# Attention and MoE on one core: squares stored in longer runs, the tile table worked out in place, the last chunk's closing dealt out, the last puts behind the branch

## Chip, core and metric

One core of a Trainium2 chip. The metric is the device time in microseconds of one execution. The engines are TensorE (PE; PEld are its weight loads), VectorE (DVE), ScalarE (ACT), GpSimd (POOL) and SyncE (SP, which here issues nearly all DMAs except the indirect ones, which are POOL's).

## The reference

```python
# attention: u, v (8, 2496, 256), z (8, 2496, 64)
scores = (1.0 / S) * np.matmul(z, z.transpose(0, 2, 1))
x = (u * np.matmul(np.maximum(scores, 0.0) ** 2, v)).reshape(B * S, D)
# MoE: N = 19968 rows, D = 256, E = 8 experts, F = 1024
logits = x @ w_gate + modality_bias[modality_id]
e_idx = np.argmax(logits, axis=1)
probs = np.exp(logits - logits.max(-1, keepdims=True))
probs /= probs.sum(-1, keepdims=True) + 1e-09
gate_w = probs[np.arange(N), e_idx]
for e in range(E):
    mask = e_idx == e
    h = np.maximum(x[mask] @ w1[e], 0.0)
    out[mask] = gate_w[mask, None] * (h @ w2[e])
```

## The kernel before

Every fp32 number of a product is split into a high and a low part in the fp32r type, and three matmuls (high x high, low x high, high x low) are summed.

**Phase 1, attention** (to 1275 us). For each of 8 batches the 2496 queries are taken in 5 chunks of 512 (the last has 448), and for each chunk the keys in 10 steps, 400 steps in all. A step makes scores s (L312), takes relu on ACT (r, L320), squares it (L366), splits the square into ah (`high`, L390, on DVE or ACT) and al (`low`, L399, DVE), and multiplies both with v into acc (L423). The square of the scores is symmetric, so 158 of the steps have their counterpart elsewhere: DVE transposes them in 32 x 32 blocks (`turn_squares`, L337, tile turn), SP stores them to DRAM (`store_squares`, L349, and L353 for a chunk's last step, i = 9), and the counterpart loads them (`load_turned`, L329) instead of computing scores. A planner with a cost for each piece ("piece" on an engine, "transfer" on SP with its number of issues) writes the order of each engine's queue.

When a chunk is done, its closing follows: the sum leaves PSUM, `weigh_u` (L490) multiplies by u, `rows_part` (L502 on ACT, L504 on DVE) and `rows_rest` (L508) make three bf16 parts, `make_rows` (L519) multiplies them by a constant matrix on PE (rows of x and gate logits), `take_rows` (L529, L530) copies those out and `take_gates` (L537) sums the logits. Routing of a batch follows: `route_logits` (L553 to L563), `route_exp` (L569), `route_places` (L577 to L598, which ends in cnt, the counts of each expert), `route_count` (L607, two small matmuls on cnt into pc), `route_gates`, `route_slots`, and `scatter` (L643, POOL) puts rows of x in DRAM by expert (xs).

**Phase 2, MoE.** Tiles of 512 rows of one expert, t = -4 to 34; the first four are tiles that are full for certain before the last batch is routed. For a tile SP fetches rows (xg, `fetch`) and a new expert's weights (wr, `fetch_weights`, split on ACT, L842, and DVE, L847); DVE transposes the rows (`turn_blocks`, L867), ACT and DVE split them (xh L874, xl L879). Eight slots f = 0 to 7 follow: `up` makes ph with six matmuls (L1246), ACT hh (L1250), DVE hl (L1251). Behind f = 3 stands the closing of the tile before (`close`: down matmuls L1264 and L1270, y on DVE L1317, `put_rows` on POOL, L1284), behind f = 7 the first half of the down matmuls. Four PSUM buffers (ps_h) serve ph, make_rows and pc in turn.

Work of the last chunk and the last batch, and the plan of the tiles (`plan`, which expert and which row each tile has), is put between the slots of tiles -4 to -1 by `put(slot, ...)`: slot n is tile -4 + n // 8, f = n % 8, and the pieces come behind that slot's matmuls. Every engine works its queue in this written order.

**The end.** The last tile's closing and a quarter tile are followed by a nest of branches (L1498, L1499) on the number of tiles left over (nq, none here). POOL issues its puts, goes over the branch, and then come the instructions that end the program (L1552).

## Time and profile before

| | |
|---|---|
| runs of the kernel | 2170.31, 2171.5, 2174.4 us; median 2171.5 |
| profiled execution | 2172.29 us, its span 2170.5 us |
| granted clock of PE, mean of the span | 0.994 |
| busy: PE / DVE / ACT / POOL | 2138.6 / 1644.4 / 1436.3 / 359.4 us |
| DMA | 356.84 MB in 563537 packets, 488818 of them under 512 bytes |

The span runs from the first to the last instruction; the execution's time has 1.8 us around it. PE is busy for 99% of it, so what is of interest is where the remaining time stands, and which engines have room at that place.

### The profile page before, as it was taken

Reading aid. Unit: us, or ns where it says so; the run is one execution under the profiler, and the core shown is the slowest. Engines: PE = TensorE matmul, PEld = TensorE weight load, DVE = VectorE, ACT = ScalarE, POOL = GpSimd, SP = SyncE. Lnnn points to the kernel's source line nnn. Section 1 sums busy time; section 2 is a strip of 40 time slices with the busy share of each in tenths; the row PEclk is TensorE's granted clock in tenths of the full one; section 3 lists DMA queues with packets and bytes.
Section 4 is the critical chain, followed back from the end, with each engine's and each line's share of the span. In section 5 each row is a group of like instructions: output and inputs, shape, how many; then the busy total and the mean of one; then the engine's idle time right before and its main releaser. Section 6 shows DMA issues by size and latency. Waiting matters only on the chain. (4 is left out here: it accounts for less than half of the span.)

```text
span 2170.5 us, 44782 instructions
## 1 busy us (share of the span) xinstructions
PE 2138.6 (99%) x17190; PEld 1858.0 (86%) x17190; DVE 1644.4 (76%) x2309; ACT 1436.3 (66%) x2021; POOL 359.4 (17%) x342
## 2 busy tenths in 40 slices
PE   9999999999999999999999989999999999999996
PEld 7888898888888998899998878888888888888885
DVE  8888889888888888788888865666666666666663
ACT  8779779779678779778688753545454545455452
POOL 0000400300300401301302303211111121212121
PEclk9999999999999999999999999999999999999998
DMA  8975965957957957947957822654545454545440
GB/s 179 260 207 115 238 188 121 260 160 141 271 141 151 287 120 155 280 116 166 264 133 166 248 54 78 200 149 136 156 130 162 124 162 121 161 131 156 137 129 24
DMA packets 563537, 356.84 MB, mean 164 GB/s; under 512 B 488818, under 2 KB 505714, under 8 KB 563314
## 3 DMA queue, kind: packets, MB, share of 16 engines
q1 hardware_dynamic: 548226, 312.82, 56.7%
q0 software_dynamic: 15088, 41.08, 5.4%
q8 instruction: 136, 2.23, 0.4%
q14 instruction: 87, 0.71, 0.1%
HBM read 229.73 MB, written 124.19 MB: 163 GB/s over the span
## 5 line engine op out<-in xcount | busy, mean ns | idle before, releaser
L423 PE MATMUL acc<-ah,vh 64*128 64x512 f32 (+1 forms) x3120 | 459.8, 385 | 2.7 <-ACT x L479 2.0
L423 PE MATMUL acc<-al,vh 64*128 64x512 f32 (+1 forms) x3120 | 448.6, 382 | 0.0
L423 PE MATMUL acc<-ah,vl 64*128 64x512 f32 (+1 forms) x3120 | 447.7, 382 | 0.0
L399 DVE TENSOR_TENSOR al<-r,ah 128x1024 fp32r<-128x1024 f32 (+1 forms) x359 | 421.9, 1186 | 32.5 <-ACT ah L390 24.0
L1251 DVE SCALAR_TENSOR_TENSOR hl<-ph,hh 128x512 fp32r<-128x512 f32 x312 | 210.1, 690 | 277.7 <-ACT hh L1250 232.7
L1246 PE MATMUL ph<-xh,w 128*128 128x512 f32 x1248 | 401.0, 392 | 0.6 <-ACT rb L530 0.6
L643 POOL DMA_INDIRECT xs<-x,sloti x160 | 201.3, 1258 | 1125.4 <-issue 582.1
L423 PEld LDWEIGHTS acc<-ah,vh 64*128 64x128 f32 x3120 | 328.5, 184 | 44.6 <-ACT x L479 4.6
L423 PEld LDWEIGHTS acc<-al,vh 64*128 64x128 f32 x3120 | 331.5, 184 | 36.4
L1250 ACT ACTIVATE hh<-ph 128x512 fp32r<-128x512 f32 x312 | 181.2, 596 | 266.8 <-PE ph L1246 213.0
L423 PEld LDWEIGHTS acc<-ah,vl 64*128 64x128 f32 x3120 | 325.7, 184 | 37.3
L390 ACT CAST ah<-r 128x1024 fp32r<-128x1024 f32 (+1 forms) x271 | 276.6, 1034 | 38.1 <-DMA r<-squares 14.2
L320 ACT ACTIVATE r<-s 128x1024 f32<-128x1024 f32 (+2 forms) x244 | 249.1, 1022 | 79.0 <-PE s L312 71.7
L1264 PE MATMUL po<-w,hh 128*128 128x512 f32 x1248 | 296.2, 389 | 0.0
L1246 PEld LDWEIGHTS ph<-xh,w 128*128 128x128 f32 x1248 | 235.7, 189 | 48.9 <-ACT rb L530 0.8
L1264 PEld LDWEIGHTS po<-w,hh 128*128 128x128 f32 x1248 | 234.0, 188 | 48.3
L1284 POOL DMA_INDIRECT out_dram<-y,ids x157 | 153.0, 975 | 668.8 <-DVE y L1317 633.0
L366 ACT ACTIVATE r<-r 128x1024 f32<-128x1024 f32 (+2 forms) x243 | 255.8, 1053 | 5.6
L1246 PE MATMUL ph<-xl,w 128*128 128x512 f32 x624 | 244.9, 392 | 3.9 <-DVE xl L879 3.9
L337 DVE STREAM_TRANSPOSE turn<-r 128x1024 f32<-128x1024 f32 x158 | 195.8, 1240 | 60.2 <-DMA squares<-turn 32.8
L312 PE MATMUL s<-zm 64*128 64x512 f32 (+1 forms) x1452 | 221.5, 397 | 1.6 <-ACT r L320 1.5
L847 DVE TENSOR_TENSOR w<-wr,w 128x1024 fp32r<-128x1024 f32 x148 | 174.7, 1220 | 17.9 <-ACT w L842 10.0
(162 smaller groups left out, 2021.8 us busy)
## 6 DMA issues: line engine op xcount, KB each, us to landing
wr<-in_moe_w_dram SPq DMA_DIRECT2D x148, 512.0 KB
squares<-turn SPq DMA_DIRECT2D x508, 128.0 KB
r<-squares SPq DMA_DIRECT2D x96, 512.0 KB
r<-squares SPq DMA_DIRECT2D x62, 448.0 KB
ut<-in_ut_dram SPq DMA_DIRECT2D x40, 512.0 KB
xg<-xs SPq DMA_DIRECT2D x156, 128.0 KB
vr<-in_v_dram SPq DMA_DIRECT2D x32, 512.0 KB
squares<-turn SPq DMA_DIRECT2D x186, 64.0 KB
```

The costliest lines, as they stand in the source:

```text
L312: nc.tensor.matmul(out=s[t][:, :w], lhsT=lhs, rhs=mv[halves[t], ql, :w], start=n == 0, stop=n == 2)
L320: nc.scalar.activation(out=r[:, t, :w], in_=s[t][:, :w] if g < 2 else s[:, :, :w], func=AF.Relu, scale=INV)
L337: nc.vector.transpose(out=y.rearrange(order, n=2), in_=st_a[g].rearrange("p n (t i) -> p n t i", i=BLK))
L366: nc.scalar.square(out=a[:, t, :w], in_=r[:, t, :w])
L390: copy(out=ah[:, :, :w], in_=st_a[g][:, :, :w])
L399: nc.vector.tensor_tensor(out=al[:, :, :w], in0=a[:, :, :w], in1=ah[:, :, :w].bitcast(F32), op=ALU.subtract)
L423: nc.tensor.matmul(out=acc[b, c][r][dh][:, :w], lhsT=V[b, k // J][y][halves[r], k % J, dh * P:(dh + 1) * P], rhs=x[halves[r], k % 2, :w], ...
L643: nc.gpsimd.indirect_dma_start(out=xs, out_offset=bass.IndirectOffsetOnAxis(ap=RT[b]["sloti"][:n, k:k + 1], axis=0), in_=x[:n, j, :], in_o ...
L1246: nc.tensor.matmul(out=ph, lhsT=lhs, rhs=rhs[:, k, :], start=n == 0, stop=n == 3 * KD - 1)
L1250: nc.scalar.activation(out=hh, in_=ph, func=AF.Relu)
L1251: nc.vector.scalar_tensor_tensor(out=hl, in0=ph, scalar=0.0, in1=hh.bitcast(F32), op0=ALU.max, op1=ALU.subtract)
L1264: nc.tensor.matmul(out=PO[t][j], lhsT=hh, rhs=both, start=f == 0, stop=False, skip_group_check=True)
```

## The change

Four things. The transposed squares lie in DRAM as `[2, P, T // QB, 2, QB]` with QB = 64, so that a row of a block is split into its even and its odd columns; DVE transposes one of two halves of a tile at a time and reads every second column; a store writes runs of 512 bytes (128 in the last step of a chunk, with twice as many DMAs), a load is contiguous. The plan's table of tiles is worked out for all tiles on every partition along the free dimension, instead of one tile on each partition and a way through DRAM with four DMAs. The closing of the last chunk moves from the head of phase 2 into slots 2 to 7 of tile -4, and the routing behind it. The last five puts are kept back until behind the branches.

```diff
-    squares = {... dram.tile([T, T], F32, ...)}
+    squares = {... dram.tile([2, P, T // QB, 2, QB], F32, ...)}
...
 def load_turned(g):
-        a = bulk.tile([P, 2, T], F32, tag="a", bufs=NA, name="r")
-        src = squares[i // 2, c, b % 2].rearrange("(s p k) q -> s p k q", s=2, k=2)
-        nc.sync.dma_start(out=a[:, :, :w], in_=src[i % 2, :, :, :w])
+        a = bulk.tile([P, T // QB, 2, QB], F32, tag="a", bufs=NA, name="r")
+        nc.sync.dma_start(out=a[:, 0:n], in_=squares[i // 2, c, b % 2][i % 2, :, 0:n])
 def turn_squares(g):
-        order = "p t (i n) -> p n t i" if i < NI - 1 else "p t (n i) -> p n t i"
-        nc.vector.transpose(out=y.rearrange(order, n=2), in_=st_a[g].rearrange("p n (t i) -> p n t i", i=BLK))
+        order = "p t r (i n) -> p n r t i" if i < NI - 1 else "p t r (n i) -> p n r t i"
+        dst = y.rearrange(order, n=2)
+        src = st_a[g].rearrange("p n (t i r) -> p n r t i", i=BLK, r=2)
+        for n in range(2):
+            nc.vector.transpose(out=dst[:, n], in_=src[:, n])
 def store_squares(g):
...
-                nc.sync.dma_start(out=dst[:, :, k0:k0 + 2 * BLK], in_=mine)
+                nc.sync.dma_start(out=dst[:, :, i % 2 * (T // QB // 2) + n], in_=mine)
             else:
                 for k in range(2 if n < 2 else 1):
-                    nc.sync.dma_start(out=dst[:, :, k0:k0 + BLK], in_=mine[:, :, k * BLK:(k + 1) * BLK])
+                    x, n0 = divmod((J // 2 + k) * P + n * BLK, QB)
+                    for r in range(2):
+                        nc.sync.dma_start(
+                            out=dst[:, :, x, r, n0:n0 + BLK], in_=mine[:, :, r, k * BLK:(k + 1) * BLK]
+                        )
+def split_view(g, x):
+        if is_turned(g):
+            return x[:, 0:w // QB].rearrange("p x t n -> p t x n")
...
 def high(g):
-        copy(out=ah[:, :, :w], in_=st_a[g][:, :, :w])
+        copy(out=split_out(g, ah), in_=split_view(g, st_a[g]))
...
 def plan():
...
-        nc.vector.tensor_scalar(out=hot, in0=end, scalar1=part, scalar2=None, op0=ALU.is_le)
+        nc.vector.tensor_tensor(out=hot, in0=wide(end), in1=at_tile.broadcast_to(shape), op=ALU.is_le)
...
-        nc.sync.dma_start(out=places, in_=placei[0:MAXT])
-        nc.sync.dma_start(out=repeats.rearrange("(m o) -> m o", o=1), in_=again[0:MAXT])
-        nc.sync.dma_start(out=repeated, in_=repeats.rearrange("(o m) -> o m", o=1).broadcast_to([P, MAXT]))
-        nc.sync.dma_start(out=meta, in_=places.rearrange("(o m) n -> o m n", o=1))
+        nc.vector.tensor_copy(out=meta[:, :, 1], in_=ex[:, :, 0])
...
-                t = piece("D", 1.18, n + 0.5, turn_squares, n, after=[high_after], take=[hold_t], drop=[hold_a])
-                stored[b, c, i] = transfer(2.8, n + 0.4, store_squares, n, issues=4 if i < NI - 1 else 6, after=[t])
+                t = piece("D", 1.3, n + 0.5, turn_squares, n, after=[high_after], take=[hold_t], drop=[hold_a])
+                stored[b, c, i] = transfer(2.2, n + 0.4, store_squares, n, issues=4 if i < NI - 1 else 6, after=[t])
...
         end = B - 1, NCH - 1
-        weigh_u(*end)
-        rows_part(*end, 0)
-        rows_rest(*end)
-        rows_part(*end, 1)
-        rows_part(*end, 2)
...
-        y = mp.tile([P, D], F32, tag="y", bufs=2 * J, name="y")
+        y = mp.tile([P, D], F32, tag="kept" if keep else "y", bufs=J + 1 if keep else J, name="y")
-        put_rows(ids, j, y)
+        if kept is None:
+            put_rows(ids, j, y)
+        else:
+            kept.append((ids, j, y))
...
-                if f == KF - 2:
+                if f == (KF - 1 if t == -EARLY else KF - 3):
                     turn_blocks(t + 1)
                     part_high(t + 1)
-                if f == KF - 1:
+                if f == (KF - 1 if t == -EARLY else KF - 2):
                     part_low(t + 1)
...
-    put(3, lambda: make_rows(*end, 0), lambda: take_rows(*end, 0, 0), lambda: take_rows(*end, 0, 1))
-    put(4, lambda: make_rows(*end, 1), lambda: take_rows(*end, 1, 0), lambda: take_rows(*end, 1, 1), lambda: take_gates(*end))
-    for slot, pieces in ((6, (route_logits, route_exp)), (7, (route_places,)), (8, (route_gates,)), (9, (route_count,)), (10, (route_slots,))):
+    put(2, lambda: weigh_u(*end), lambda: rows_part(*end, 0))
+    put(4, lambda: rows_rest(*end), lambda: rows_part(*end, 1))
+    put(5, lambda: rows_part(*end, 2))
+    put(7, lambda: make_rows(*end, 0), lambda: take_rows(*end, 0, 0), lambda: take_rows(*end, 0, 1))
+    put(7, lambda: make_rows(*end, 1), lambda: take_rows(*end, 1, 0), lambda: take_rows(*end, 1, 1), lambda: take_gates(*end))
+    for slot, pieces in ((8, (route_logits, route_exp)), (9, (route_places,)), (9, (route_gates,)), (9, (route_count,)), (10, (route_slots,))):
...
-    put(21, lambda: prefetch(-1), lambda: fetch_weights(0))
+    put(17, lambda: fetch_weights(0))
+    put(21, lambda: prefetch(-1))
...
-        finish(end_of, j, ids, PO[end_of][j])
+        finish(end_of, j, ids, PO[end_of][j], kept)
...
+    for k in kept:
+        put_rows(*k)
```

What this makes of the written order, at three places. First DVE from the head of tile -4: hl are the slots' differences, w the weights' low parts, x and rb the last chunk's closing, lg its gate logits; before:

```order
L490 TENSOR_TENSOR x<-x,ut 128x4x256
L508 TENSOR_TENSOR x<-x,rb 128x4x256
L1251 SCALAR_TENSOR_TENSOR hl<-ph,hh 128x512
L847 TENSOR_TENSOR w_0_18960<-wr,w_0_18960 128x4x256
L504 TENSOR_TENSOR rb<-x,rb 128x1024
L1251 SCALAR_TENSOR_TENSOR hl<-ph,hh 128x512
L847 TENSOR_TENSOR w_0_18960<-wr,w_0_18960 128x4x256
L1251 SCALAR_TENSOR_TENSOR hl<-ph,hh 128x512 x3
L537 TENSOR_REDUCE lg<-rb 128x32
L1251 SCALAR_TENSOR_TENSOR hl<-ph,hh 128x512 x2
```

and now:

```order
L1259 SCALAR_TENSOR_TENSOR hl<-ph,hh 128x512
L860 TENSOR_TENSOR w_0_19309<-wr,w_0_19309 128x4x256
L1259 SCALAR_TENSOR_TENSOR hl<-ph,hh 128x512
L860 TENSOR_TENSOR w_0_19309<-wr,w_0_19309 128x4x256
L1259 SCALAR_TENSOR_TENSOR hl<-ph,hh 128x512
L508 TENSOR_TENSOR x<-x,ut 128x4x256
L1259 SCALAR_TENSOR_TENSOR hl<-ph,hh 128x512 x2
L526 TENSOR_TENSOR x<-x,rb 128x4x256
L1259 SCALAR_TENSOR_TENSOR hl<-ph,hh 128x512
L522 TENSOR_TENSOR rb<-x,rb 128x1024
L1259 SCALAR_TENSOR_TENSOR hl<-ph,hh 128x512 x2
L555 TENSOR_REDUCE lg<-rb 128x32
```

The closing's multiplication by u and its parts stood ahead of the first hl and now stand between hl2 and hl6, with the weight differences ahead of them.

Second, DVE a little later, from the sum of the gate logits to cnt; before:

```order
L563 TENSOR_TENSOR sh<-lg,mx 128x96
L867 STREAM_TRANSPOSE xt<-xg 128x1024
L1251 SCALAR_TENSOR_TENSOR hl<-ph,hh 128x512
L577 SCALAR_TENSOR_TENSOR val<-sh,em_126 128x96
L579 TENSOR_REDUCE idx<-val 128x12
L582 MEMSET hot 128x160
L583 TENSOR_TENSOR hot<-idx,em_126 128x12x8
L587 MEMSET hot 64x8
L589 SCALAR_TENSOR_TENSOR run<-reset,hot 128x160
L598 CAST cnt<-run 128x8
L879 TENSOR_TENSOR xl<-xt,xh 128x1024
L1251 SCALAR_TENSOR_TENSOR hl<-ph,hh 128x512
```

and now:

```order
L880 STREAM_TRANSPOSE xt<-xg 128x1024
L892 TENSOR_TENSOR xl<-xt,xh 128x1024
L1259 SCALAR_TENSOR_TENSOR hl<-ph,hh 128x512
L571 TENSOR_TENSOR bias<-brow,mod_148 128x96
L577 TENSOR_TENSOR lg<-lg,bias 128x96
L571 TENSOR_TENSOR bias<-brow,mod_149 128x96
L577 TENSOR_TENSOR lg<-lg,bias 128x96
L579 TENSOR_REDUCE mx<-lg 128x12
L581 TENSOR_TENSOR sh<-lg,mx 128x96
L1259 SCALAR_TENSOR_TENSOR hl<-ph,hh 128x512
L595 SCALAR_TENSOR_TENSOR val<-sh,em_124 128x96
L597 TENSOR_REDUCE idx<-val 128x12
```

The transpose xt and the difference xl of tile -3 now stand ahead of all routing, and the routing between and behind the first two hl of tile -3; the cast to cnt follows five rows further on. On PE the two matmuls on cnt stand behind the twelve matmuls of slots 0 and 1 of tile -3 in both kernels.

Third, SP from the plan's table on, where xg are rows of a tile and wr weights; before:

```order
L762 DMA places<-p_placei 42x2
L763 DMA repeats<-p_again 42x1
L764 DMA repeated<-repeats 128x42
L765 DMA meta<-places 1x84
L788 TENSOR_LOAD meta
L788 ISA x2
L801 ISA
L801 DMA xg<-xs 32x16x64
```

and now:

```order
L815 ISA
L815 DMA gate<-xs 128x4x2
L831 TENSOR_LOAD meta
L831 ISA x2
L840 ISA
L840 DMA wr<-in_moe_w_dram 128x1024
L840 ISA
L840 DMA wr<-in_moe_w_dram 128x1024
```

The weights' issues come directly behind the last rows of tile -2, once the table can be read; the rows of tile -1 follow them, where before the rows of tiles -1 and 0 stood ahead of the weights. POOL's queue has its last five puts ahead of the branches before, and behind them now.

## Rows read from the trace of the kernel before

**Rows 1.** The page, its first part: busy time in us (share of the span) and instructions of each engine.
```profile
PE 2138.6 (99%) x17190; PEld 1858.0 (86%) x17190; DVE 1644.4 (76%) x2309; ACT 1436.3 (66%) x2021; POOL 359.4 (17%) x342
```

**Rows 2.** Stretches of the span: from:to, length in us; busy time (x instructions) of PE, of its weight loads (PEld), DVE, ACT and POOL; granted clock of PE; share of the DMA engines; GB/s.
```profile
0.00:1275.00 1275.00, 1267.24 (x12738) 1113.71 (x12739) 1081.63 (x1450) 1008.21 (x1352) 194.30 (x173) 1.00 0.74 187
1275.00:1350.00 75.00, 68.93 (x365) 57.27 (x364) 46.39 (x131) 25.28 (x50) 19.83 (x20) 0.93 0.26 64
1350.00:2150.00 800.00, 798.44 (x4068) 683.68 (x4068) 514.62 (x724) 401.59 (x618) 141.63 (x146) 1.00 0.48 142
2150.00:2171.00 21.00, 4.00 (x24) 3.31 (x22) 1.73 (x5) 1.26 (x3) 3.60 (x4) 0.65 0.09 28
```

**Rows 3.** What PE waited for in phase 1, 0 to 1275: line, releaser, us in total, times, the longest.
```profile
PE po L519 <- DVE rb L504: 2.1, 3, 0.9
PE acc L423 <- ACT x L479: 2.0, 3, 1.1
PE s L312 <- ACT r L320: 1.5, 1, 1.5
PE warm L1119 <- POOL zeros L102: 1.0, 1, 1.0
PE acc L423 <- DVE ah L373: 0.7, 1, 0.7
```

**Rows 4.** PE in order of time, at the places where it sat idle behind phase 1: start and duration in us, engine, line, operation, out<-in, shapes; in brackets the idle time before it and what ended that.
```profile
1279.22 0.39 PE L1246 MATMUL ph<-xl,w 128*128 128x512 f32 x1
...
1279.90 0.39 PE L1246 MATMUL ph<-xl,w 128*128 128x512 f32 x1
...
1281.02 0.20 PE L519 MATMUL po<-mover,rb 64*128 64x88 bf16 x1 [0.51 <-DVE hl L1251]
1283.88 1.04 PE L519 MATMUL po<-mover,rb 64*128 64x88 bf16 x23 [2.67 <-DVE hl L1251]
1285.48 0.79 PE L1246 MATMUL ph<-xh,w 128*128 128x512 f32 x1 [0.56 <-ACT rb L530]
...
1301.79 0.50 PE L1246 MATMUL ph<-xl,w 128*128 128x512 f32 x1 [2.34 <-DVE xl L879]
...
1371.51 0.50 PE L1246 MATMUL ph<-xl,w 128*128 128x512 f32 x1 [1.56 <-DVE xl L879]
```

**Rows 5.** Stretches of 5 us in the hand-over, columns as in rows 2; the granted clock is the number behind the last bracket.
```profile
1285.00:1290.00 5.00, 4.52 (x33) 3.27 (x34) 1.85 (x3) 2.01 (x8) 0.00 (x0) 0.56 0.00 0
...
1300.00:1305.00 5.00, 3.21 (x10) 2.58 (x11) 2.73 (x6) 0.60 (x1) 0.00 (x0) 0.80 0.10 10
1305.00:1310.00 5.00, 5.00 (x21) 4.12 (x21) 2.14 (x6) 2.22 (x4) 0.00 (x0) 0.86 0.00 0
```

**Rows 6.** POOL's last puts in order of time (columns as in rows 4), and the instructions of the branch (L1499) and of the program's end (L1552) that hold no work: engine's queue, operation, count, durations in ns (min/median/max), first and last start in us.
```profile
2147.44 0.97 POOL L1284 DMA_INDIRECT out_dram<-y,ids  x1 [11.71 <-DVE y L1317]
...
2155.31 0.97 POOL L1284 DMA_INDIRECT out_dram<-y,ids  x1 [0.43 <-DVE y L1317]
...
L1499 DVEq EVENT_SEMAPHORE  x1: 21/21/21, 2158.7 to 2158.7; - x1
L1499 POOLq INC_SWDGE_SEM  x1: 2206/2206/2206, 2159.1 to 2159.1; - x1
...
L1552 SPq EVENT_SEMAPHORE  x14: 17/28/28, 2161.3 to 2170.5; - x14
...
L1552 POOLq DRAIN  x3: 40/107/8313, 2161.4 to 2170.2; - x3
```

**Rows 7.** The store issues of the squares (tile turn, on SP), their transposes on DVE, and the transpose of the MoE rows (xt): durations in ns (min/median/max), first and last start, shapes.
```profile
L349 SPq DMA_DIRECT2D squares<-turn x508: 302/554/2449, 18.5 to 1211.0; - x170
L353 SPq DMA_DIRECT2D squares<-turn x186: 303/526/3027, 49.6 to 1220.4; - x186
L337 DVE STREAM_TRANSPOSE turn<-r x158: 1203/1240/1251, 17.2 to 1216.4; 128x1024 f32<-128x1024 f32 x158
...
L867 DVE STREAM_TRANSPOSE xt<-xg x40: 435/1235/1245, 1242.8 to 2124.0; 128x1024 f32<-128x1024 f32 x39, 128x256 f32<-128x256 f32 x1
```

**Rows 8.** DVE and then ACT in the hand-over, in order of time, columns as in rows 4.
```profile
1280.28 0.68 DVE L1251 SCALAR_TENSOR_TENSOR hl<-ph,hh 128x512 fp32r<-128x512 f32 x1
...
1282.01 1.22 DVE L504 TENSOR_TENSOR rb<-x,rb 128x1024 bf16<-128x1024 f32 x1
...
1293.60 0.25 DVE L553 TENSOR_TENSOR bias<-brow,mod 128x96 f32<-128x96 f32 x1
...
1298.68 0.25 DVE L577 SCALAR_TENSOR_TENSOR val<-sh,em 128x96 f32<-128x96 f32 x1
...
1300.44 0.17 DVE L598 CAST cnt<-run 128x8 fp32r<-128x8 f32 x1
...
1295.34 0.28 ACT L569 ACTIVATE ex<-sh 128x96 f32<-128x96 f32 x1 [2.37 <-DVE sh L563]
...
1297.45 0.59 ACT L1250 ACTIVATE hh<-ph 128x512 fp32r<-128x512 f32 x1
```

**Rows 9.** SP's DMA issues around the plan's table, and ACT's first cast of tile 0's weights, in order of time, columns as in rows 4.
```profile
1331.57 0.39 SPq L762 DMA_DIRECT2D places<-p_placei  x1
...
1353.40 4.33 SPq L827 DMA_DIRECT2D wr<-in_moe_w_dram  x5
...
1357.49 1.05 ACT L842 CAST w<-wr 128x1024 fp32r<-128x1024 f32 x1 [3.68 <-DMA wr<-in_moe_w_dram]
```

More of the change, by code (lines that the diff above doesn't have):

```diff
@@ L69, in tile_attention_moe @@
     xs = dram.tile([E * CAP, XW], F32, name="xs")
-    places = dram.tile([MAXT, 2], I32, name="places")
-    repeats = dram.tile([MAXT], F32, name="repeats")
-    squares = {(q, c, e): dram.tile([T, T], F32, name=f"squares{q}_{c}_{e}") for q, c in pairs for e in range(2)}
+    squares = {(q, c, e): dram.tile([2, P, T // QB, 2, QB], F32, name=f"squares{q}_{c}_{e}") for q, c in pairs for e in range(2)}
     ident_r = const.tile([P, P], F32R, name="ident")
     ident = ident_r.bitcast(F32)
-    meta = const.tile([1, MAXT, 2], I32, name="meta")
     nq = const.tile([1, 1], I32, name="nq")
@@ L82, in tile_attention_moe @@
     repeated = small.tile([P, MAXT], F32, name="repeated")
+    meta = small.tile([P, MAXT, 2], I32, name="meta")
     ph1, feed = ExitStack(), ExitStack()
@@ L398, in low @@
         if i < NI - 1:
[L399 removed]
+            nc.vector.tensor_tensor(
+                out=split_out(g, al), in0=split_view(g, a), in1=split_out(g, ah).bitcast(F32), op=ALU.subtract
+            )
         else:
@@ L699, in plan @@
         nc.vector.tensor_tensor_scan(out=end, data0=ones[:, 0:E].bitcast(F32), data1=tiles, initial=0.0, op0=ALU.mult, op1=ALU.add)
-        of_expert = t8("p_of", 3, E)
+        of_expert = t8("p_of", 2, E)
         beg, fin = of_expert[:, 0], of_expert[:, 1]
-        nc.vector.tensor_tensor(out=beg, in0=end, in1=tiles, op=ALU.subtract)
+        start = t8("p_start")
+        nc.vector.tensor_tensor(out=start, in0=end, in1=tiles, op=ALU.subtract)
+        nc.vector.scalar_tensor_tensor(out=beg, in0=start, scalar=float(-T), in1=skip, op0=ALU.mult, op1=ALU.add)
         nc.vector.scalar_tensor_tensor(out=fin, in0=cnt, scalar=float(-T), in1=skip, op0=ALU.add, op1=ALU.add)
-        nc.vector.tensor_copy(out=of_expert[:, 2], in_=skip)
         total = end[:, E - 1:E]
@@ L729, in plan @@
         yield
-        place = t8("p_place", 2)
-        row, ex = place[:, 0:1], place[:, 1:2]
-        hot = t8("p_hot")
-        nc.vector.tensor_scalar(out=hot, in0=end, scalar1=part, scalar2=None, op0=ALU.is_le)
+        shape = [P, MAXT, E]
+        wide = lambda x: x.rearrange("p (o e) -> p o e", o=1).broadcast_to(shape)
+        hot, mine = (mp.tile(shape, F32, tag=n, bufs=1, name=n) for n in ("p_hot", "p_mine"))
+        ex, ex8 = (mp.tile([P, MAXT, 1], F32, tag=n, bufs=1, name=n) for n in ("p_ex", "p_ex8"))
@@ L740, in plan @@
-        mine = t8("p_mine", 3, E)
-        nc.vector.tensor_tensor(
-            out=mine, in0=of_expert, in1=hot.rearrange("p (o e) -> p o e", o=1).broadcast_to([P, 3, E]), op=ALU.mult
-        )
-        picked = t8("p_picked", 3, 1)
-        nc.vector.tensor_reduce(out=picked, in_=mine, axis=AX.X, op=ALU.add)
-        yield
-        beg, last, off = (picked[:, n] for n in range(3))
-        nc.vector.tensor_scalar(out=row, in0=part, scalar1=beg, scalar2=float(T), op0=ALU.subtract, op1=ALU.mult)
@@ L749, in plan @@
-        nc.vector.tensor_tensor(out=row, in0=row, in1=off, op=ALU.add)
-        here = t8("p_here", 1)
-        nc.vector.tensor_scalar(out=here, in0=part, scalar1=total, scalar2=-1.0, op0=ALU.subtract, op1=ALU.is_equal)
+        nc.vector.tensor_tensor(out=hot, in0=wide(em8), in1=ex8.broadcast_to(shape), op=ALU.is_equal)
+        yield
+        picked = [mp.tile([P, MAXT, 1], F32, tag=f"p_at{n}", bufs=1, name="p_at") for n in range(2)]
+        for n, x in enumerate((beg, fin)):
+            nc.vector.tensor_tensor(out=mine, in0=wide(x), in1=hot, op=ALU.mult)
+            nc.vector.tensor_reduce(out=picked[n], in_=mine, axis=AX.X, op=ALU.add)
@@ L752, in plan @@
+        yield
+        row, last = (x[:, :, 0] for x in picked)
+        nc.vector.scalar_tensor_tensor(out=row, in0=number, scalar=float(T), in1=row, op0=ALU.mult, op1=ALU.add)
+        here = mp.tile([P, MAXT], F32, tag="p_here", bufs=1, name="p_here")
+        nc.vector.tensor_scalar(out=here, in0=number, scalar1=total, scalar2=-1.0, op0=ALU.subtract, op1=ALU.is_equal)
         nc.vector.tensor_scalar(out=here, in0=here, scalar1=odd[:, 2:3], scalar2=float(P), op0=ALU.mult, op1=ALU.mult)
```

50 lines of the change are left out of this document (27 added, 23 removed).

## The prediction

> **What bounds the kernel now.** First the busy times of the page: TensorE (PE) is busy 2138.6 us, VectorE (DVE) 1644.4 [rows 1]; the last semaphore is passed at 2170.5 [rows 6]. So about 32 us of the span are open to any change that takes no matmul away, and the order of the work on each engine shows none taken away or added. Second the stretches [rows 2]: in phase 1 (to 1275) PE idles 7.8 us, in the hand-over (1275 to 1350) 6.1, in the MoE tiles (to 2150) 1.6, and the rest lies behind 2154: from 2150 on it is busy 4.0 us and no more. Third what PE waits for in phase 1 [rows 3]: 1.0 is the warm-up and 1.5 the first root, both at the start; what remains to be gained between them and 1275 is some 5 us. DVE is idle there 193 us, ACT 267. A cheaper store, DVE pass or load can therefore win a few microseconds at most in phase 1, but it can lose more.
>
> Fourth the single idle times of PE behind phase 1 [rows 4]: 0.51, 2.67 and 0.56 around make_rows of the last chunk, 2.34 before tile -3 (it waits for xl), 1.56 before tile 0 (again xl), together 7.64. Fifth the granted clock: 0.56 of full speed in 1285 to 1290, 0.80 and 0.86 in the two stretches from 1300 [rows 5]. PE was busy nearly all of the first and last, so the low level (1.2 GHz) cost about 5 x 0.44 + 5 x 0.20 + 5 x 0.14 = 3.9, a little less since part of 1300 to 1302 was idle. Each of the two falls came right behind one of the two longest idle times.
>
> Sixth the end [rows 6]: the last put of output rows is issued from 2155.31 for 0.97, to 2156.28. POOL then goes over the branch of L1498 and does its closing instruction (INC_SWDGE_SEM) from 2159.1 for 2.2; only at 2161.4 does its DRAIN begin, which lasts 8.3, and at 2170.5 the last semaphore is passed. SyncE (SP) passes its first semaphore there at 2161.3, and DVE lands behind the branch at 2158.7.
>
> **The change, part by part.**
>
> *Squares in 512-byte runs.* DVE transposes 158 tiles of 1024 elements, 1240 ns each [rows 7]. Each becomes two of 512 that read every second element. The transpose of xt takes 1235 at 1024 elements and 435 at 256 [rows 7], so 512 lie on the line between them at 435 + 800/3 = 702, and a pair costs 1.40: +0.16 x 158 = 26 us of DVE. No row shows a transpose that reads with a stride. The bounds are a pair at 1.24 (no cost; both halves overlap) and at 2.48 (every read at half pace), +196 us. I take 1.40, since the writes of the present transposes already skip every second element in most steps and their longest is 1251, as fast as the contiguous xt. The 26 us are hidden by DVE's 193 idle ones. Without that cover each pair would delay its chunk by its 0.16. The Trainium skill, "SBUF — State Buffer", section "Door 1: The DMA port swizzle", says that SBUF is read in lines of 16 bytes and that two hits in a line are enough for full pace. By that rule every second fp32 costs nothing and the sum stays as it is; no run here shows such a transpose yet.
>
> SP: of the store issues, 508 have the size of an ordinary step and 186 that of a last step of a chunk [rows 7], six for each of 31 last steps. These become twelve: 186 x 0.526 = 98 us more of issue in phase 1, about 3.2 for each last step, and the planner still counts six. SP is one queue: behind those issues stand the loads of squares, ut, v and xg. An ordinary step keeps four issues. Casts and differences of turned tiles read as many elements as before, in runs of 64, so I leave their price. For phase 1 I take +0.5, from -3 (most of what [rows 3] leaves) to +4 (a few late loads).
>
> *The last chunk's closing dealt out.* I follow the row prices. A slot of six matmuls takes 1.36 us (three start in 0.68 [rows 4]), and slot 3 of tile -4 ends at 1280.3, as before. Before, DVE did weigh_u, the parts and hl in a row, and make_rows stood behind slots 3 and 4. Now both make_rows stand behind slot 7, with parts between the hl. PE runs slots 4 to 7 with 0.34 of wait (the last ph needs hl3 read) and is free at 1280.3 + 4 x 1.36 + 0.34 = 1286.1. DVE and ACT are not ready. weigh_u, behind three hl and two weight differences, ends at 1282.2. ACT's cast of part 0 (1024 elements, as in [rows 9], 1.05) ends at 1283.2, and two hh of 0.6 follow it there. hl3 and hl4 (0.68 each [rows 8]) end at 1285.0; rows_rest, a tensor op like the 1.22 one of L504 [rows 8], ends at 1286.3; ACT's cast of part 1 at 1287.3; hh5 and hl5 at 1288.5; part 2 at 1289.7. So PE waits 3.6 where it waited 2.67. The second half then needs hl7's buffer: 0.7.
>
> With make_rows' 24 matmuls twice (23 took 1.04 at the low clock [rows 4], half of that at the full one) and the down matmuls (16 at 0.227 and 16 of half the columns, 5.5), tile -3's f0 ends at 1298.3. It no longer waits for xl, which is made under the down matmuls: -2.34. But route_logits, route_exp and route_places now stand in its slots 0 and 1, and PE's two matmuls on cnt (route_count) stand right behind slot 1. Before, cnt was ready before them. Now: f0's matmuls, hh 0.59 on ACT, hl 0.68, the six small ops of route_logits (0.25 like the one at 1293.60, and 0.03 between, 1.7 us in all), exp 0.28 on ACT, hh1 0.59 behind it, hl1 0.68, then route_places, from 1298.68 to 1300.61, 1.9 [rows 8]. From the end of f0 at 1298.3 that makes 0.6 + 0.7 + 1.7 + 0.3 + 0.6 + 0.7 + 1.9 = 6.5, so cnt is there at about 1304.9, while PE comes free behind f1 at 1299.7: 5.2 us of wait, and behind it stand all of f2 to f7. Sum of the new waits: 0.34 + 3.6 + 0.7 + 5.2 = 9.8.
>
> Clock: I expect two falls again, behind the 3.6 and behind the 5.2, at the price that the present two show, 3.9, give or take 1.
>
> *Table in place.* Four DMAs go (places, repeats, repeated, meta, the first at 1331.57 [rows 9]), and the weights of tile 0 are asked for in front of the rows of tiles -1 and 0 instead of behind both. They now leave SP at 1353.4, and ACT, which waits 3.68 for them, casts the first 4.1 us later [rows 9]; that makes tile 0's turn late and gives PE's 1.56. Asked for when the table is done, at about 1335 by the first of the four DMAs, they are there by 1340; the turn also stands a slot earlier. So the 1.56 goes. The table's DVE ops grow to 336 elements, about 0.5 us each (on the line from 0.25 for 96 elements to 1.22 for 1024 [rows 8]), a dozen of them; DVE is idle a third of [rows 2]'s third stretch.
>
> Net of the hand-over: 9.8 - 7.64 = +2.2, rounded to +2 since part of the removed waits stood at the low clock; with the clock's +/-1 and as much for the walk, 0 to +4.
>
> *Last puts behind the branch.* POOL has nothing to do in the 11.7 us ahead of 2147.4 [rows 6]; there it goes over the branch and does INC, under matmuls. Five puts follow, the last again at 2155.31 to 2156.28, and DRAIN can start there instead of at 2161.4: -5.1 if DRAIN keeps its 8.3. DVE's landing (2158.7) lies inside those 8.3, and SP's semaphore comes with POOL's. Bounds: 0 and -10.6 (below). *y buffers*, eight to four: four puts of 0.97 fall to a tile, and with 36 tiles in the third stretch a buffer comes round once in 22 us; nothing.
>
> Sum against the profiled execution, 2172.3 (its span 2170.5 and 1.8 around it; the median of the three runs is 0.8 lower): 2172.3 + 0.5 + 2 - 5.1 = 2169.7, and 2169 beside the median. A measurement here tells about 0.2% (4.3 us) from no change: faster is below 2167.2, slower above 2175.8.
>
> **The rivals.**
>
> *A: DRAIN is short.* At 8.3 us it is long because INC and the puts stood just ahead of it. With INC long done it takes a fraction of one, and the end is set by DVE's landing at 2158.7 and SP: about 2160 instead of 2170.5, -10.6, total 2172.3 + 2.5 - 10.6 = 2164. For it: INC itself took 2.2 here, so POOL's closing instructions do depend on what is outstanding. Against it: DRAIN began 5 us behind the last put's end, and it still took 8.3.
>
> *B: the end hangs on the last put.* DRAIN waits for that put's whole chain, whatever stands between; the end stays 14.2 us behind the put: total 2174 to 2175.
>
> *C: slower, by late loads in phase 1.* Place: SP behind each of the 31 last steps, where six unplanned issues take 3.2 us. If the loads that stand behind them then come late, ah, al and in the end acc wait. The price is up to 31 x 3.2 = 98. The point from which it decides: 6.3 us, the distance from 2169.5 to 2175.8, or 0.2 us on average for each last step. A third of the last steps passing on 1.5 us gives 2185. For it: the planner does not know of the issues, and single ones of them took 3.0 us [rows 7]. Against: none of PE's waits in [rows 3] is for a load of squares, so there is slack between load and use.
>
> *D: the longer runs pay.* Half the packets free DMA engines, loads come earlier, and phase 1 gains. [Rows 3] cap it at some 5 us; -3 gives 2166. The Trainium skill, "DMA: Bandwidth & Descriptors", section "Specifications", asks for at least 512 bytes for full pace and says that smaller writes are read, changed and written back. By that rule the stores take half their DMA time or less; the idle time of PE that the trace shows in phase 1 leaves it the same few microseconds.
>
> **How the numbers follow.** The forecast holds with 0.55 (2166 to 2173), A 0.14, B 0.10, C 0.15, D 0.06. Faster: A, D and about a quarter of the forecast's own spread, 0.14 + 0.06 + 0.14 = 0.34. Slower: C and a fifth of B, 0.17. The same: 0.49. The range, 2162 to 2176, holds A, B, D and the forecast, and leaves out C and a little of A.
>
> **What would show it.** After: PE idle 3 to 4 us before the first make_rows matmul and about 5 before the matmul on cnt, two falls of the clock near them, none before tile 0; turn at about 0.70 a half; INC before 2145, DRAIN right behind the last put and 8.3 long. Wrong would be: a DRAIN of under 1 us (A), one that begins later than the put ends (B), waits of PE for ah or al of turned steps in phase 1 (C), or cnt ready in time.

## The result, and the profile after

The changed kernel takes 2184.04 us (median of four runs, 2181.0 to 2184.97), the kernel before 2170.9 beside it: a ratio of 1.0056, with a 95% interval of 1.0038 to 1.0073. It is slower by 12 to 13 us, where 2169 was forecast with a range from 2162 to 2176. The profiled execution, the shortest of the four, took 2181.0 us, its span 2179.2; that is 8.7 above the profiled execution of the kernel before.

The first part of the page, against [rows 1]:

```profile
PE 2153.3 (99%) x17190; PEld 1882.9 (86%) x17190; DVE 1654.5 (76%) x2463; ACT 1444.1 (66%) x2027; POOL 362.6 (17%) x343
```

The same number of matmuls (17190) keeps PE busy for 2153.3 us instead of 2138.6. That is 14.7 more, and it is more than the whole loss. PE does not wait more: it runs longer. The stretches, columns as in [rows 2], say where:

```profile
0.00:1275.00 1275.00, 1268.74 (x12748) 1139.45 (x12749) 1089.36 (x1611) 1016.21 (x1361) 197.69 (x174) 1.00 0.68 188
1275.00:1350.00 75.00, 66.78 (x348) 55.02 (x347) 46.39 (x124) 24.00 (x45) 19.94 (x20) 0.91 0.28 80
1350.00:2150.00 800.00, 800.00 (x3998) 673.18 (x3998) 511.35 (x715) 396.77 (x609) 140.10 (x144) 1.00 0.48 139
2150.00:2180.00 30.00, 17.78 (x101) 15.23 (x99) 7.38 (x15) 7.09 (x12) 4.86 (x5) 0.83 0.08 27
```

Phase 1 is no worse. In the third stretch PE is busy for all of its 800 us and starts 3998 matmuls, where [rows 2] has 4068 with 1.6 us of idle time. The granted clock is 1.00 in both. So each matmul takes longer, though nothing is waited for. Two halves of a tile in order of time show it most plainly, first of the kernel before, then of the changed one (start, duration, engine, line, operation):

```profile
1387.86 3.79 PE L1264 MATMUL po<-w,hh 128*128 128x512 f32 x16
1391.48 2.08 PE L1270 MATMUL po<-w,hl 128*128 128x256 f32 x16
...
1398.86 3.79 PE L1264 MATMUL po<-w,hh 128*128 128x512 f32 x16
```

```profile
1388.30 3.89 PE L1272 MATMUL po<-w,hh 128*128 128x512 f32 x16
1392.03 2.06 PE L1278 MATMUL po<-w,hl 128*128 128x256 f32 x16
...
1399.50 3.89 PE L1272 MATMUL po<-w,hh 128*128 128x512 f32 x16
```

Sixteen 512-column matmuls take 3.79 us before and 3.89 after, and from one such group to the next it is 11.00 and 11.20 us. From start to start that is (1391.48 - 1387.86)/16 = 226 ns and (1392.03 - 1388.30)/16 = 233 ns. The mean distance between starts over the 512-column matmuls of phase 2 is 227.4 before and 232.6 after, and it is so from the first tile to the last. The 256-column ones are a trace faster (2.06 against 2.08). A tile has two such halves: 2 x 0.20 = 0.40 us, or 14 for the 36 tiles or so of the third stretch.

The hand-over's waits of PE, which answer to [rows 4]:

```profile
1273.61 0.47 PE L1254 MATMUL ph<-xh,w 128*128 128x512 f32 x1 [0.56 <-DVE x L501]
...
1285.85 0.30 PE L537 MATMUL po<-mover,rb 64*128 64x88 bf16 x3 [2.07 <-DVE hl L1259]
1286.99 0.98 PE L537 MATMUL po<-mover,rb 64*128 64x88 bf16 x21 [0.84 <-DVE rb L522]
1288.18 1.03 PE L537 MATMUL po<-mover,rb 64*128 64x88 bf16 x23 [0.21 <-DVE hl L1259]
...
1304.46 0.35 PE L625 MATMUL pc<-cnt,below 128*128 128x8 f32 x1 [5.10 <-DVE sm L645]
```

The wait before the matmul on cnt is 5.10; those of make_rows are 2.07, 0.84 and 0.21. The bracket of the first names sm, but DVE shows that the matmul waited for cnt, which ends at 1304.31, while sm still runs when the matmul starts at 1304.46:

```profile
1304.14 0.17 DVE L616 CAST cnt<-run 128x8 fp32r<-128x8 f32 x1
1304.23 0.24 DVE L645 TENSOR_REDUCE sm<-ex 128x12 f32<-128x96 f32 x1
```

The 0.56 at 1273.61, in tile -4's first matmuls, is new. No wait on xl is left, neither before tile -3 nor before tile 0. The granted clock fell twice again (columns as in [rows 5]):

```profile
1285.00:1290.00 5.00, 3.10 (x49) 2.48 (x49) 3.02 (x4) 2.77 (x11) 0.00 (x0) 0.57 0.00 0
1290.00:1295.00 5.00, 5.00 (x20) 4.01 (x20) 3.24 (x3) 1.20 (x3) 0.00 (x0) 0.75 0.35 69
...
1305.00:1310.00 5.00, 5.00 (x14) 3.94 (x14) 2.61 (x6) 1.64 (x2) 0.00 (x0) 0.54 0.01 3
```

The end, as in [rows 6], and the transposes and stores, as in [rows 7]:

```profile
2169.09 0.97 POOL L1292 DMA_INDIRECT out_dram<-y,ids  x1 [0.44 <-DVE y L1326]
...
L1516 POOLq INC_SWDGE_SEM  x1: 2106/2106/2106, 2152.7 to 2152.7; - x1
...
L1571 SPq EVENT_SEMAPHORE  x14: 17/28/28, 2166.1 to 2179.2; - x14
...
L1571 POOLq DRAIN  x3: 40/113/9527, 2168.9 to 2179.0; - x3
```

```profile
L350 SPq DMA_DIRECT2D squares<-turn x508: 302/467/1884, 18.3 to 1205.3; - x170
L355 SPq DMA_DIRECT2D squares<-turn x372: 302/449/1579, 47.7 to 1217.0; - x186
L339 DVE STREAM_TRANSPOSE turn<-r x316: 658/690/750, 17.0 to 1211.6; 128x512 f32<-128x512 f32 x158
```

INC_SWDGE_SEM ran at 2152.7, under matmuls. The last put ends at 2170.06 and POOL's DRAIN, in the trace from 2168.9 for 9.5 us, is over 8.3 us behind that. The span ends 9.1 us behind the last put, where it was 14.2.

### The profile page after: what moved, and what is told of

It is laid out like the page before. It is cut to its first block, busy times and chain, and to the rows that moved or that the text cites. A ratio compares the mean times of both kernels' runs of the same rounds, so it can differ in the third digit from the quotient of the medians.

```text
span 2179.2 us, 45148 instructions
## 1 busy us (share of the span) xinstructions
PE 2153.3 (99%) x17190; PEld 1882.9 (86%) x17190; DVE 1654.5 (76%) x2463; ACT 1444.1 (66%) x2027; POOL 362.6 (17%) x343
## 5 line engine op out<-in xcount | busy, mean ns | idle before, releaser
L1254 PE MATMUL ph<-xh,w 128*128 128x512 f32 x1248 | 406.0, 396 | 0.6 <-DVE x L501 0.6
L441 PEld LDWEIGHTS acc<-ah,vh 64*128 64x128 f32 x3120 | 334.0, 184 | 35.3 <-ACT x L497 1.7
L441 PEld LDWEIGHTS acc<-al,vh 64*128 64x128 f32 x3120 | 336.2, 184 | 29.5
L441 PEld LDWEIGHTS acc<-ah,vl 64*128 64x128 f32 x3120 | 330.7, 184 | 30.5
L1272 PE MATMUL po<-w,hh 128*128 128x512 f32 x1248 | 305.5, 396 | 0.0
L406 ACT CAST ah<-r 128x1024 fp32r<-128x1024 f32 (+1 forms) x277 | 281.9, 1033 | 30.5 <-PE acc L441 19.7
L339 DVE STREAM_TRANSPOSE turn<-r 128x512 f32<-128x512 f32 x316 | 205.6, 690 | 38.0 <-DMA squares<-turn 24.8
```

Source lines behind the costliest of these rows:

```text
L339: nc.vector.transpose(out=dst[:, n], in_=src[:, n])
L406: copy(out=split_out(g, ah), in_=split_view(g, st_a[g]))
L441: nc.tensor.matmul(out=acc[b, c][r][dh][:, :w], lhsT=V[b, k // J][y][halves[r], k % J, dh * P:(dh + 1) * P], rhs=x[halves[r], k % 2, :w], ...
L1254: nc.tensor.matmul(out=ph, lhsT=lhs, rhs=rhs[:, k, :], start=n == 0, stop=n == 3 * KD - 1)
L1272: nc.tensor.matmul(out=PO[t][j], lhsT=hh, rhs=both, start=f == 0, stop=False, skip_group_check=True)
```

## The experiments

Apart from make_rows in the hand-over, the order of the work on PE in phase 2 is the same in both kernels, and so are the operands' shapes. What differs is where they lie. A tile's address in SBUF is the sum of the sizes ahead of it, and the change alters small ones (meta moves, number is new, the plan's small tiles go). The start addresses in bytes per partition, from the allocation of the two built kernels, with the remainder of 256 behind them:

```
                              before            after
xh, xl (first buffer)         25920  (64)       25792 (192)
hh     (first buffer)         84800  (64)       84672 (192)
hl     (first buffer)        101184  (64)      101056 (192)
weights, first buffer (w1)   192320  (64)      192320  (64)
weights, second buffer (w1)  132160  (64)      136768  (64)
ah / vh of phase 1     158528 / 109376 (64)   158400 / 109248 (192)
```

Buffers of one kind follow each other in multiples of 2048 bytes. Theory P (placement): a matmul of phase 2 is slowed when its two operands, one loaded into PE ahead of it and the other streamed through, start at different remainders. (In `up` the expert's weights are loaded and the rows streamed; in the down matmuls on hh it is the hidden values that are loaded and the weights that are streamed.) In phase 1, ah and vh moved together, and its pace did not change. Theory C (contention or order): something in the new order slows PE. The kernel has padding tiles named room, which make it easy to move one thing alone.

**e1: rows and both weight buffers back to one remainder.**

```diff
-    small.tile([P, 24], F32, name="room")
+    small.tile([P, 56], F32, name="room")
-    wp.tile([P, 16], F32, name="room")
+    wp.tile([P, 48], F32, name="room")
```

> The changed kernel with two padding tiles each 128 bytes longer per partition (small's room 24 to 56 floats, wp's room 16 to 48), so that the MoE rows (xh, xl), the hidden values (hh, hl) and both weight buffers start at the same remainder of 256 bytes, as in the kernel before; order and work are those of the changed kernel. Theory P (placement: the 512-column matmuls of phase 2 take 232.6 ns instead of 227.3 from start to start because rows and weights lie 128 bytes apart in that remainder): the pace is 227 again, some 14 us come back, the profiled span is about 2165 and the time 2167 to 2170. Theory C (contention or order: the new order, the fewer y buffers or the table slow the matmuls): the pace stays at 232 to 233 and the time at 2181 to 2185.

Measured: 2166.66 us (12 runs), ratio to the kernel before 0.9974 (0.9963 to 0.9985). Its third and fourth stretch, and two groups of down matmuls:

```profile
1350.00:2150.00 800.00, 800.00 (x4080) 685.41 (x4079) 513.42 (x722) 401.53 (x617) 140.10 (x144) 1.00 0.48 139
2150.00:2180.00 30.00, 6.73 (x39) 5.70 (x37) 3.45 (x8) 2.30 (x5) 4.86 (x5) 0.82 0.07 24
...
1390.58 3.79 PE L1272 MATMUL po<-w,hh 128*128 128x512 f32 x16
...
1401.59 3.79 PE L1272 MATMUL po<-w,hh 128*128 128x512 f32 x16
```

Now 4080 matmuls start in the same 800 us, and sixteen take 3.79 again. Two padding tiles, which no instruction touches, bring back the pace and with it all of the loss. From the first matmul of tile -4 to the end of the last one the profiled executions took 896.4 us in the changed kernel (1271.38 to 2167.78) and 881.0 in e1 (1275.73 to 2156.73), with nearly the same waits: the pace is worth some 15 us. The medians lie 17 apart; the rest is not accounted for. Theory C is out. The profiled span was 2168.2 rather than the expected 2165, since phase 1 ended 4.4 us later than in the changed kernel's profile, whose phase 1 has the same instructions; single executions differ that much there.

**e2 and e3: only one of the two weight buffers at a distance.** e2 lengthens only small's room of the changed kernel, e3 does the same to the kernel before.

```diff
-    small.tile([P, 24], F32, name="room")
+    small.tile([P, 56], F32, name="room")
```

> The changed kernel with only small's room 128 bytes longer: xh, xl, hh and hl are back at the remainder 64 of 256 that the first weight buffer (even steps of the tiles) has, but the second weight buffer moves along to 192. Theory P: tiles on the first weight buffer run at 227 ns per 512-column matmul, those on the second at 232 to 233, alternating tile by tile; the time lies half way, about 2174 to 2177. Theory C: all tiles at 232 to 233, 2181 to 2185.

> The kernel before with small's room 128 bytes longer and nothing else: rows, hidden values and the second weight buffer move from the remainder 64 of 256 to 192, the first weight buffer stays at 64. Theory P: tiles on the first weight buffer slow down to 232 to 233 ns per 512-column matmul, those on the second stay at 227; about 7 us slower than the kernel before, 2177 to 2179. Theory C: no change, 2169 to 2174.

Measured: 2172.42 and 2176.32 us, one run each. The groups of sixteen down matmuls, of e2 and then of e3:

```profile
1386.29 3.88 PE L1272 MATMUL po<-w,hh 128*128 128x512 f32 x16
...
1397.34 3.89 PE L1272 MATMUL po<-w,hh 128*128 128x512 f32 x16
...
1408.44 3.79 PE L1272 MATMUL po<-w,hh 128*128 128x512 f32 x16
...
1419.55 3.82 PE L1272 MATMUL po<-w,hh 128*128 128x512 f32 x16
```

```profile
1384.79 3.79 PE L1264 MATMUL po<-w,hh 128*128 128x512 f32 x16
...
1395.90 3.82 PE L1264 MATMUL po<-w,hh 128*128 128x512 f32 x16
...
1407.05 3.88 PE L1264 MATMUL po<-w,hh 128*128 128x512 f32 x16
...
1418.10 3.89 PE L1264 MATMUL po<-w,hh 128*128 128x512 f32 x16
```

Two groups at 3.88 to 3.89 and two at 3.79 to 3.82 follow each other, as the tiles change from one weight buffer to the other. In e3 the code is that of the kernel before, instruction by instruction. At 1386 and 1397 us the weights come from the second buffer, later from the first: e2 is slow on the second and e3 on the first, each time the buffer whose remainder differs from that of the rows. The groups at 3.82 are closings of the tiles on the fast buffer; by the written order they stand between the up matmuls of the next tile, which is on the slow one. Why that costs them 0.03 us is not shown. Theory P's times were 2 us high for e2 and 1 for e3, which is less than single executions differ in phase 1 alone; its alternation came.

**e4, e10 and e11: which distances.** e4 and e11 lengthen both padding tiles of the changed kernel by 64 and by 96 bytes instead of 128; e10 takes e3 and moves the first weight buffer along too (head's room 40 to 72 floats), so that all lie at 192.

> The changed kernel with both padding tiles 64 bytes longer: rows and hidden values at the remainder 0 of 256, the first weight buffer at 64, the second at 192; they lie 192 and 64 bytes apart. Theory P, if what counts is whether both start at the same remainder of 128 bytes or more: slow on both (232 or more); if only a distance of 128 collides: 227 on both and about 2168 in all. Theory C: 2181 to 2185.

> The kernel of e3 with the first weight buffer moved down by 128 bytes as well (the room tile of the head pool 40 to 72 floats): rows, hidden values and both weight buffers now all start at the remainder 192 of 256, where the kernel before has all at 64. If it is the distance between the two operands that counts: 227 ns per 512-column matmul in every tile, 2169 to 2174, like the kernel before. If it is the remainder of the rows or weights itself: 232 to 233 everywhere, some 2184.

> The changed kernel with both padding tiles 96 bytes longer: rows and hidden values at the remainder 32 of 256, the first weight buffer at 64, the second at 0, so 32 bytes apart either way. If every distance that is no multiple of 256 costs (64, 128 and 192 did): 231 to 233 ns in all tiles, 2178 to 2184. If a distance under 64 bytes is as good as none: 227 and 2166 to 2170.

Measured, one run each: e4 2177.91, e10 2172.29, e11 2182.14 us. Groups of sixteen of e4, e10 and e11:

```profile
1401.70 3.89 PE L1272 MATMUL po<-w,hh 128*128 128x512 f32 x16
...
1412.92 3.83 PE L1272 MATMUL po<-w,hh 128*128 128x512 f32 x16
```

```profile
1398.65 3.79 PE L1264 MATMUL po<-w,hh 128*128 128x512 f32 x16
...
1409.66 3.79 PE L1264 MATMUL po<-w,hh 128*128 128x512 f32 x16
```

```profile
1399.62 3.89 PE L1272 MATMUL po<-w,hh 128*128 128x512 f32 x16
...
1410.85 3.89 PE L1272 MATMUL po<-w,hh 128*128 128x512 f32 x16
```

With everything at 192 the pace is that of the kernel before, so the remainder itself does not matter. The two operands' distance does: 32 bytes apart, either way, is as bad as 128, and of 64 and 192, the two that alternate in e4, one costs as much (233 ns, the first buffer, whose weights start 64 above the rows' remainder) and the other under half of it (229 to 230, the second, 192 above). In the kernel before the two weight buffers differ by an odd multiple of 256, and both are fast. So of the distances tried only multiples of 256 are free, odd ones too.

**e5 to e8: the change's own parts, each undone or moved in e1.** These four ran on one chip, and their medians are best compared with each other. e5 puts the last five puts ahead of the branches again:

```diff
+    for k in kept:
+        put_rows(*k)
     if over:
         parts = nc.values_load(nq[0:1, 0:1], min_val=0, max_val=4 * MAXT)
...
-    for k in kept:
-        put_rows(*k)
```

> The realigned kernel (e1) with one part undone: the last five puts stand ahead of the branches again. Theory T (DRAIN takes 8.3 us from POOL's last work, and the branch and INC_SWDGE_SEM stood between the last put and it): the end moves from 11.4 to 16.5 us behind the last matmul, +5.1 us against e1, about 2171 to 2172, no different from the kernel before. Rival (the end hangs on the put itself): no change against e1, 2166 to 2167.

Measured: 2172.61 us, ratio 1.0014 (1.0003 to 1.0025), 6.0 above e1's median (on another chip). Its last put and DRAIN:

```profile
2154.76 0.97 POOL L1292 DMA_INDIRECT out_dram<-y,ids  x1 [0.43 <-DVE y L1326]
...
L1572 POOLq DRAIN  x3: 40/107/8313, 2160.8 to 2169.6; - x3
```

The put ends at 2155.73, DRAIN begins 5.0 us later and the span ends 14.2 behind the put (2169.9), as in the kernel before. From the last matmul's end to the span's it is 16.5 us, and 11.4 in e1. The 5.1 us are the branch and INC, and DRAIN keeps its 8.3 either way.

e6 puts the closing back, and the transpose of tile -3's rows one slot ahead as before (code shortened):

```diff
         end = B - 1, NCH - 1
+        weigh_u(*end)
+        rows_part(*end, 0)
+        rows_rest(*end)
+        rows_part(*end, 1)
+        rows_part(*end, 2)
...
-                if f == (KF - 1 if t == -EARLY else KF - 3):
+                if f == (KF - 2 if t == -EARLY else KF - 3):
...
-    put(2, lambda: weigh_u(*end), lambda: rows_part(*end, 0))
-    put(4, lambda: rows_rest(*end), lambda: rows_part(*end, 1))
-    put(5, lambda: rows_part(*end, 2))
-    put(7, lambda: make_rows(*end, 0), ...)
-    put(7, lambda: make_rows(*end, 1), ...)
-    for slot, pieces in ((8, (route_logits, route_exp)), (9, (route_places,)), (9, (route_gates,)), (9, (route_count,)), ...):
+    put(3, lambda: make_rows(*end, 0), ...)
+    put(4, lambda: make_rows(*end, 1), ...)
+    for slot, pieces in ((6, (route_logits, route_exp)), (7, (route_places,)), (8, (route_gates,)), (9, (route_count,)), ...):
```

> The realigned kernel (e1) with the last chunk's closing and the routing back in the places that they had in the kernel before (weigh_u and the parts ahead of tile -4, make_rows behind slots 3 and 4, routing behind 6 to 10). By the waits of the traces: e1 waits 2.24 + 0.90 + 0.40 + 5.14 = 8.7 us there, the kernel before 0.51 + 2.67 + 0.56 + 2.34 = 6.1; so 2 to 3 us less than e1, about 2164, if the dealt-out closing costs what its waits show. If dealing out helps elsewhere (an earlier start of tile -4 or fewer falls of the clock): the same as e1 or up to 3 us more.

Measured: 2163.9 us, ratio 0.9974 (0.9964 to 0.9984). PE's waits there:

```profile
1281.73 0.63 PE L537 MATMUL po<-mover,rb 64*128 64x88 bf16 x23 [2.53 <-DVE hl L1264]
1282.94 0.79 PE L1259 MATMUL ph<-xh,w 128*128 128x512 f32 x1 [0.58 <-ACT rb L548]
...
1300.38 0.50 PE L1259 MATMUL ph<-xl,w 128*128 128x512 f32 x1 [2.34 <-DVE xl L892]
```

They are the three long ones of [rows 4] again (2.53, 0.58, 2.34), without tile 0's. Against e1 the medians say 2.8 us less, the ratios nothing; those two ran on different chips. Against e5 on the same chip it is 8.7 less, of which 5.1 are the puts. The traces show the place: from the first matmul of tile -4 to that of tile 0 it is 94.1 us (1272.46 to 1366.55), and 98.4 in e1 (1275.73 to 1374.11). So dealing out closing and routing in this way costs about 3 to 4 us rather than bringing any.

e7 leaves the closing and moves the routing:

```diff
-    for slot, pieces in ((8, (route_logits, route_exp)), (9, (route_places,)), (9, (route_gates,)), (9, (route_count,)), (10, (route_slots,))):
+    for slot, pieces in ((7, (route_logits, route_exp)), (8, (route_places,)), (9, (route_gates,)), (10, (route_count,)), (10, (route_slots,))):
```

> The realigned kernel (e1) with the routing's pieces put elsewhere: route_logits and route_exp behind make_rows (slot 7, ahead of tile -3's transpose), route_places behind slot 8, route_count behind slot 10 instead of 9. If the 5.1 us before the matmul on cnt is the chain hl0, logits, exp, hh1, hl1, places: cnt is ready 2 to 3 us earlier and is asked for 1.4 us later, the wait is under 1.5 us, and the fall of the clock behind it goes as well: 4 to 7 us less than e1, 2160 to 2163. If the wait only moves (to xl of tile -3, which now stands behind the logits): within 2 us of e1.

Measured: 2159.69 us, ratio 0.9956 (0.994 to 0.9973). The two waits of tile -3:

```profile
1295.85 0.50 PE L1254 MATMUL ph<-xl,w 128*128 128x512 f32 x1 [0.48 <-DVE xl L892]
...
1300.64 0.24 PE L625 MATMUL pc<-cnt,below 128*128 128x8 f32 x1 [0.64 <-DVE cnt L616]
```

The wait before cnt's matmul shrinks from 5.14 to 0.64, and xl of tile -3 costs 0.48. From tile -4's first matmul to tile 0's it is 91.9 us (1270.98 to 1362.90), 6.5 less than in e1. So the chain that makes cnt was the wait's cause, and the wait did not merely move.

e8 takes back the squares' storage (layout, the single transpose, the stores and the planner's two costs as before).

> The realigned kernel (e1) with the squares stored as in the kernel before (runs of 256 and 128 bytes, one transpose of 1024 elements, the planner's costs of before). If the longer runs bring nothing to a phase bound by the matmuls: within 1.5 us of e1, 2165 to 2168. If they brought the 1 to 4 us by which phase 1 ended earlier in the traces of the changed order: 2168 to 2171.

Measured: 2169.45 us, ratio 0.9995 (0.9985 to 1.0005), against e1's 0.9974. On the same chip as e5 it is 3.2 less, of which 5.1 are the puts: by that the longer runs are worth 1.9 us, by the medians beside e1 2.8 and by the ratios 1.0 (against e5) or 4.6 (against e1). So a gain of a few microseconds is likely, but it is hardly clear of noise, and the profile of e8 doesn't show it: phase 1 ended at 1272.97, where the nine profiles with the new storage lie between 1269.92 and 1275.73. e8 takes back layout, transposes, stores and planner's costs together; which of them counts is not shown. PE's wait of 0.6 us at tile -4's start, which e1, e5, e6, e7 and e9 share with the changed kernel, is gone in e8.

**e9: the closing spread so that DVE keeps up,** on top of e7.

```diff
         end = B - 1, NCH - 1
+        weigh_u(*end)
...
-    put(0, lambda: part_weights_low(-1, KD))
-    put(1, lambda: part_weights_low(-1, KD + 1))
-    put(2, lambda: weigh_u(*end), lambda: rows_part(*end, 0))
-    put(4, lambda: rows_rest(*end), lambda: rows_part(*end, 1))
-    put(5, lambda: rows_part(*end, 2))
+    put(0, lambda: rows_part(*end, 0))
+    put(1, lambda: rows_rest(*end))
+    put(2, lambda: rows_part(*end, 1))
+    put(3, lambda: rows_part(*end, 2))
+    put(5, lambda: part_weights_low(-1, KD))
+    put(9, lambda: part_weights_low(-1, KD + 1))
```

> The kernel of e7 with the last chunk's closing spread otherwise: weigh_u ahead of tile -4, the parts behind slots 0 to 3, the weights' differences behind slots 5 and 9 instead of 0 and 1. If the waits before make_rows in e7 (2.23 + 0.90 + 0.21) come from the late parts and hl in DVE's queue, they shrink to 1 to 2 us: 1 to 3 us less than e7, 2157 to 2159. If DVE is simply full from tile -4's start to make_rows, whatever the order: within 1 us of e7.

Measured: 2158.4 us, ratio to the kernel before 0.9937 (0.9924 to 0.9951). PE's waits and the hand-over's stretch:

```profile
1284.48 0.20 PE L537 MATMUL po<-mover,rb 64*128 64x88 bf16 x1 [0.65 <-DVE hl L1260]
1285.07 0.63 PE L537 MATMUL po<-mover,rb 64*128 64x88 bf16 x23 [0.40 <-DVE hl L1260]
...
1297.58 0.24 PE L625 MATMUL pc<-cnt,below 128*128 128x8 f32 x1 [0.64 <-DVE cnt L616]
...
1275.00:1350.00 75.00, 72.49 (x404) 60.76 (x403) 52.28 (x135) 28.68 (x55) 20.94 (x21) 1.00 0.37 100
```

The waits before make_rows are 1.05 in all instead of 3.3, xl of tile -3 costs 0.76, and the granted clock stays at 1.00 through the hand-over: with no wait above 0.76 left in it, the clock does not fall. From tile -4's first matmul to tile 0's it is 88.7 us (1271.22 to 1359.93), 3.2 less than in e7; the medians, from different chips, lie 1.3 apart. This is the fastest of the kernels here, some 14 us under the one before and, on another chip, 26 under the changed one.

## Why the prediction was wrong

The step that failed stands in the first paragraph: since PE idled for only 1.6 us in the MoE tiles [rows 2] and the order took no matmul away, I let that stretch stand in the sum as it was. It had no term for the pace of a matmul that waits for nothing. That term was +14 to +15 us. No view of the kernel before could show it. The diff could have raised the question, though not given the price: it changes the size of tiles ahead of xh and hh and leaves the first weight buffer where it is, in a kernel that carries four padding tiles. None of the rivals held it either; C had the kernel slower, but by late loads in phase 1, and no wait of PE for them came.

Beside that the steps can be held against the runs one by one:

- *Transposes.* A half took 690 ns (702 expected). The rule of the Trainium skill, "SBUF — State Buffer", section "Door 1: The DMA port swizzle", that two hits in a line of 16 bytes are enough, agrees: beside the 702 worked out for a contiguous half, reading every second fp32 cost nothing visible. On DVE all transposes together rose by 9.8 us, from 195.8 to 205.6, where 26 were expected:

```profile
L337 DVE STREAM_TRANSPOSE turn<-r 128x1024 f32<-128x1024 f32 x158 | 195.8, 1240 | 60.2 <-DMA squares<-turn 32.8 <-ACT r L366 21.1 <-issue 3.6
L339 DVE STREAM_TRANSPOSE turn<-r 128x512 f32<-128x512 f32 x316 | 205.6, 690 | 38.0 <-DMA squares<-turn 24.8 <-ACT r L383 9.2 <-issue 2.3
```

- *SP's issues.* 372 instead of 186, but at a median of 449 ns instead of 526, so by the forecast's reckoning 69 us more rather than 98. That reckoning left out that the 508 ordinary issues got shorter too (median 554 to 467). Added up over the trace, the store issues took 474 us before and 445 now: SP got freer, not busier. No load came late for PE, and rival C had no place.
- *Phase 1.* Forecast +0.5 within -3 to +4. In the two profiles tile -4 begins 3.2 us earlier (1274.62 and 1271.38), and e8 says about -1 to -5, hardly clear of noise. If that gain holds, rival D was right in direction. Its half of the stores' DMA time did not come: a packet of 256 bytes took 21.7 ns on average before, one of 512 takes 34.7 now.
- *Hand-over.* Forecast waits 0.34 + 3.6 + 0.7 + 5.2 = 9.8, found 2.07 + 0.84 + 0.21 + 5.10 = 8.2, and the 0.56 at tile -4's start, which the forecast lacked. The walk was right on cnt to 0.1 and about 1.5 long on make_rows. The clock fell twice, as expected, and stayed low for longer: by the prediction's reckoning the three rows above cost 5.7 against 3.9, less what PE idled in them. From tile -4's first matmul to tile 0's e1 takes 98.4 us and the kernel before 94.9 (1274.62 to 1369.56), +3.4; e6 puts the cost of the dealt-out closing and routing at 3 to 4.
- *Tile 0.* The 1.56 is gone, as forecast. From tile 0's first matmul to the last one's end e1 takes 1.8 us less than the kernel before. Together with the +3.4 that is +1.6, where +2 was forecast.
- *The end.* Forecast -5.1, and the traces show 14.2 and 9.1 us behind the last put; e5 takes it back. Rivals A and B fall: DRAIN has its 8.3 us with and without INC just ahead of it, and the end moved against the put. A's argument from INC's 2.2 us does not hold either: ahead of the last puts, under matmuls, it took 2.1.

Summed between the two profiled executions: 15.4 for the pace (the changed kernel against e1, from tile -4's first matmul on), -3.2 in phase 1, +3.4 in the hand-over, -1.8 behind it and -5.1 at the end are +8.7, which is what lies between 2181.0 and 2172.3. The medians are another 4 us apart, and where these lie is not shown. With the pace as before, e1, the time is 2166.7, inside the range and 2 us under the forecast. That is less than phase 1 differs by between single profiles, so the nearness of this total shows less than the terms do.
